# Block 0 of a gated long convolution with a GLU in a new written order: filter basis, condition and loads

## The chip, the cores and the metric

The kernel runs on one core of a Trainium2 chip. The metric is the device time of one execution in microseconds (us); lower is better. A core has TensorE (matrix products; in the profile PE, and PEld for its weight loads), VectorE (DVE), ScalarE (ACT), GpSimd (POOL) and SyncE (SP), which here only issues DMAs.

## The reference, cut to what matters

All data is bf16, with 2048 rows (S), a width D of 576 and a hidden width F of 4608.

```python
mod = silu(c) @ w_mod                        # (1, 6 * 576): sa, ca, ga, sb, cb, gb
h   = layernorm(q) * (1 + ca) + sa
k_shift[s] = sum over t of k[s - 3 + t] * shift_k[:, 3 - t]      # four taps
kv  = k_shift * v
y   = irfft2(rfft2(kv, zero-padded to 4096) * rfft2(ssm_k, padded))[:2048]   # causal long convolution
y   = y + kv * ssm_D
x   = q + ga * (h * y)
h2  = layernorm(x) * (1 + cb) + sb
out = x + gb * ((silu(h2 @ w1) * (h2 @ w3)) @ w2)
```

The condition `c` is one row of 576. Its six products with `w_mod` are needed once, before any row of the result can be finished.

## The kernel before

**Blocks.** The 2048 rows are cut into 8 blocks of 256. For a block, `x_spectrum` multiplies the shifted and gated rows `kv` by a basis of cosines and sines (`Fb`) on TensorE; `w_spectrum` does the same for a block of the filter (`kT`, with the basis `Fk`), each in groups of products whose result is copied out of PSUM. VectorE multiplies the spectra of the blocks that meet in one output block and adds them (`pair`, tiles p and z), and TensorE turns the sum back (`inverse`). A layernorm, the gate and the residual follow; then h2 is written as rows (`h2row`), transposed to columns (`h2T`; by TensorE for blocks 0 and 1, by a transposing DMA in `turn_all` for the others) and modulated by `cbcol` and `sbcol` (1 + cb and sb as columns; `modulate`).

**The GLU.** Four groups of 512 rows, two blocks each, run through `stream(r)` (products of h2T with w1 and w3, which pass through the buffers `wst`) and `down(r)` (products with w2, whose result VectorE multiplies by `gbrow` into `og` and adds to x). Block 0 alone starts the first stream; block 1 joins it later. The convolution of blocks 2 and 3 belongs to the time of stream and down 0, and so on, so that the stream of a group waits for the h2T of its two blocks: the hand-over.

**Two kinds of order.** Nothing is issued at once: each call is recorded, and line 208 (`_Op.emit`), which therefore stands behind every row of the profile, issues it at the end. `setup`, `early_loads` and `first_block` (all of block 0) are emitted in the order in which they are written, engine by engine. From `rec.fixed = False` in `run` on, a planner decides. `weigh` gives each step a due time, `plan` lays the steps out by a model of their lengths, and `search` repeats that `TRIES` times with other random numbers: noise on the due times (`NOISE`), and one of `HOLDS` for how early a load may be issued ahead of its due time. It keeps the order whose modelled time, a mean over the three `CASES`, is smallest. The model adds `WAKE`, 26 ns, from the end of one step to the start of another that waits for it (`lag`). The streams' products are "lanes", whose order is given; all other TensorE work of the planned part is set between them.

**Block 0, step by step.** `setup` makes angles with iotas and integer arithmetic (`angles`, two sets: 1 for the filter basis, 0 for the others) and takes them modulo 2048 (`whole_turns`); ScalarE turns them into bases by sine (`wave`). `taps_waves` makes `Fk`: its first half by sine, its second half as the first times a column of signs, on GpSimd. `early_loads` issues the loads on SP's queue and on ScalarE's; `load_mod(m)` and `load_mod_tail` fetch w_mod's six parts (in the order ga, ca, sa, cb, sb; `load_gb` fetches gb's later). `first_block` then writes, for TensorE: blank products (`warm`); `shift_taps`, which spreads the four taps over the partitions with products of one row; blank products; the filter's spectrum `w_spectrum(0)` between `shifted_rows` (k times the taps on VectorE, shifted and summed by 16 products with a moved identity); `cond` (the silu of c, a row, as five one-row products of 128 columns, which repeat it over 128 columns of `crep`); 16 products of `x_spectrum(0)`; the modulations `mod_piece(2)`, `(1)` and `(0)` (crep times a part of w_mod, 10 products each) around the 24 products of the inverse; `mod_piece(4)` and `(3)` in `mod_columns`, whose rows become columns by twelve small products with four columns each, in two steps of six; the transposes of h2row; and the filter spectrum of block 1.

The blank products and the order of these steps are all that the change touches by hand. Around it stand, on VectorE: k times the taps (p), `kv`, the sums X and V of the spectra and their products z, hg (normalised and gated rows), the residual and the layernorm statistics (`ln_sum` on ScalarE into a tile called junk, `quick_stats`, `ln_square`, `ln_rest`, `ln_bias`).

Of the kernel before, what the change touches and what calls it, by code (L numbers as in the profile page):

```python
# [10 lines left out]
BF16 = mybir.dt.bfloat16  # L11
# [227 lines left out]
class _Recorder:  # L239
# [12 lines left out]
    DOUBT = 900.0  # L252
    PATIENCE = 900.0
    FETCH = 256
    TRIES = 40
    NOISE = 1500.0
    HOLDS = (25000.0, 35000.0, 45000.0, 60000.0)
# [176 lines left out]
    def lag(self, u, v, exact):  # L434
        if v.engine == "sync" and not u.lane and not u.fixed and not exact:
            return v.end + self.DOUBT

        if u.engine == "tensor" and v.engine == "tensor" and v.swap is not u:
            return v.start
        return v.end + self.WAKE  # L440

    def search(self):
# [7 lines left out]
        for n in range(self.TRIES):  # L450
            dice = random.Random(n)
            hold = dice.choice(self.HOLDS) if n else self.HOLD
            for u in self.units:
                u.latest = u.wish + (dice.gauss(0.0, self.NOISE) if n and not u.lane else 0.0)
            try:
                order = self.plan(hold)[1]
            except AssertionError:
                continue
            took = [self.plan(hold, order, *case)[0] for case in self.CASES]
            mean = sum(took) / len(took)  # L460
            if best is None or mean < best[0]:
                best = mean, order
# [242 lines left out]
class _Kernel:  # L705
# [30 lines left out]
    def setup(self):  # L736
# [38 lines left out]
        self.sign = self.small.tile([P, 1], F32, name="sign", tag="sign", bufs=1)  # L775
# [10 lines left out]
        nc.vector.memset(self.one[:], 1.0)  # L786
        nc.vector.tensor_copy(self.acol[:, 0:4], coli[:, 0:4])
        self.ang = {}
        self.angles(nc.vector, 1)
        self.whole_turns(1)  # L790
        nc.vector.tensor_single_scalar(coli[:, 6:7], coli[:, 6:7], 1, op=ALU.bitwise_and)
        nc.vector.tensor_copy(self.acol[:, 4:7], coli[:, 4:7])
        nc.vector.tensor_scalar(self.sign[:], self.acol[:, 6:7], -2.0, 1.0, op0=ALU.mult, op1=ALU.add)
        self.angles(nc.gpsimd, 0)
        nc.gpsimd.memset(self.moved[:, 0:2], 0.0)
        nc.gpsimd.run(lambda: make_identity(self.tc.nc, self.ident), 900.0, (self.ident,))

    def early_loads(self):
        nc = self.nc
        self.crow = self.hp.tile([1, D], BF16, name="crow", tag="u")  # L800
# [3 lines left out]
        self.k0 = self.ld.tile([P, 2, D], BF16, name="kh", tag="kh")  # L804
        nc.scalar.dma_start(self.k0[:], self.k[0:B, :].rearrange("(p c) d -> p c d", c=2))
        nc.scalar.dma_start(self.drow, self.ssm_D.rearrange("(o n) -> o n", o=1))
        self.load_taps(0)
        nc.sync.dma_start(self.crow[:], self.c)
# [3 lines left out]
        self.load_x(0)  # L812
# [28 lines left out]
    def angles(self, engine, which):  # L841
        n = 3 - which
        ang = self.spec.tile([P, n, 2, P], I32, name="ang", tag="V")
        for x in range(n):
# [4 lines left out]
        self.ang[which] = ang  # L849

    def whole_turns(self, which):
        part = self.ang[which][:]
# [6 lines left out]
    def taps_waves(self):  # L859
        self.wave(self.Fk[:, 0:2], self.ang[1][:], 1)  # L860
        self.nc.gpsimd.tensor_scalar(self.Fk[:, 2:4], self.Fk[:, 0:2], self.sign[:, 0:1], 0.0,
                                     op0=ALU.mult, op1=ALU.add)

    def forward_waves(self):
        self.wave(self.Fb[:, 0:2], self.ang[0][:, 0:2], 1)
        self.wave(self.Fb[:, 2:3], self.ang[0][:, 1:2], -1)
# [5 lines left out]
    def inverse_sums(self):  # L872
        nc = self.nc
        for lo, hi, at in ((0, 1, 0), (3, 5, 1)):
            n = hi - lo
            nc.gpsimd.tensor_add(self.Fi[:, at:at + n, 0], self.Fb[:, lo:hi, 0], self.Fb[:, lo:hi, 1])
            nc.gpsimd.tensor_scalar(self.Fi[:, at:at + n, 1], self.Fb[:, lo:hi, 0], -1.0, 0.0,
                                    op0=ALU.mult, op1=ALU.add)
# [14 lines left out]
    def shift_taps(self):  # L893

        nc = self.nc
        for q, (lo, n) in enumerate(((0, 256), (256, 160), (416, 160))):
# [3 lines left out]
            for h in range(2):  # L900
                nc.tensor.matmul(ps[:, h, 0:2 * n], self.one[at, :],
                                 self.shk_raw[at, first + 2 * n * h:first + 2 * n * (h + 1)], start=True, stop=True)
            src = ps[:, :, 0:2 * n].rearrange("p h (d j) -> p j h d", j=4)
# [6 lines left out]
    def cond_silu(self):  # L910
        self.sc = self.hp.tile([1, D], BF16, name="sc", tag="u")
        self.nc.scalar.activation(self.sc[:], self.crow[:], ACT.Silu)

    def cond(self):

        nc, sc = self.nc, self.sc
        self.crep = self.hp.tile([P, 5, P], BF16, name="crep", tag="u")
        pt = self.ps()
        ptv = pt[:].rearrange("p a b -> p (a b)")
        for ct in range(5):  # L920
            n = min(P, D - ct * P)
            nc.tensor.matmul(ptv[:n, ct * P:(ct + 1) * P], sc[0:1, ct * P:ct * P + n], self.one[0:1, :],
                             start=True, stop=True)
        nc.scalar.copy(self.crep[:, 0:4, :], pt[:, 0, :].rearrange("p (a b) -> p a b", a=4))
        nc.scalar.copy(self.crep[0:64, 4, :], pt[0:64, 1, 0:P])
# [13 lines left out]
    def mod_piece(self, m):  # L939
        nc = self.nc  # L940
        p = self.mod_products(m)
# [14 lines left out]
    def mod_columns(self):  # L956
# [8 lines left out]
        for i in range(2):  # L965
            self.warm(1 + i, self.shk[:, 0, 0:512], ps)
# [6 lines left out]
        self.warm(1, self.shk[:, 0, 0:512], ps)  # L973
# [61 lines left out]
    def forward(self, basis, rhs, dst, more=()):  # L1035

        nc = self.nc
        for e in range(2):
            for cs in range(2):
# [3 lines left out]
                if more and e + cs == 0:  # L1043
                    nc.vector.tensor_copy(out, ps[:, :, 0:H])
                else:
                    nc.scalar.copy(out, ps[:, :, 0:H])
# [320 lines left out]
    def first_block(self):  # L1367
# [4 lines left out]
        self.warm(4, blank)  # L1372
        self.shift_taps()
        self.whole_turns(0)
        self.taps_waves()
        self.forward_waves()
        self.cond_silu()
        self.inverse_waves()
        self.warm(6, blank)
        rows = self.shifted_rows()  # L1380
        next(rows)
        spectrum = self.w_spectrum(0)
        next(spectrum)
        next(rows)
        next(spectrum)
        next(rows)
        self.run_all(rows)
        self.cond()
        self.run_all(spectrum)
        self.load_taps(1)  # L1390
        mean, rstd = self.quick_stats(x1[:, 0, :], "l1")
        nmr = self.small.tile([P, 1], F32, name="l1nm", tag="nmr2")
        nc.gpsimd.tensor_mul(nmr[:], mean, rstd)
        nc.gpsimd.tensor_single_scalar(nmr[:], nmr[:], -1.0, op=ALU.mult)
        self.run_all(self.x_spectrum(0))
        self.inverse_sums()
# [4 lines left out]
        self.load_gb()  # L1401
# [3 lines left out]
        ssum, ssq = [self.small.tile([P, 1], F32, name="l1" + k, tag=t) for k, t in (("s", "ssum"), ("q", "ssq"))]  # L1405
        self.ln_sum(x1, 1, 0, ssum[:])
        self.ln_sum(x1, 1, 1, ssq[:])
        self.mod_piece(2)
        nc.vector.tensor_add(X[:, 0, :], X[:, 1, :], X[:, 2, :])
        nc.vector.tensor_mul(z[:, 0:3, :], X[:, 0:3, :], V[:, 0:3, :])  # L1410
        var = self.ln_square(ssum)
        nc.vector.tensor_add(X[:, 3, :], X[:, 4, :], X[:, 5, :])
        r = self.ln_rest(ssq, var)
        nc.scalar.activation(hg[:, 0, :], x1[:, 0, :], ACT.Identity, bias=nmr[:, 0:1], scale=rstd[:, 0:1])
        nc.vector.tensor_mul(z[:, 3:6, :], X[:, 3:6, :], V[:, 3:6, :])
        b = self.ln_bias(ssum, r)
# [16 lines left out]
        nc.scalar.copy(y[:, 0, :].rearrange("p (h d) -> p h d", h=2), ps[0][:, :, 0:H])  # L1433
        nc.vector.tensor_mul(hg[:, 0, :], hg[:, 0, :], y[:, 0, :])
        nc.vector.tensor_add(x1[:, 0, :], x1[:, 0, :], hg[:, 0, :])
        self.residual_row(0, 1, ps[1])
# [3 lines left out]
        columns = self.mod_columns()  # L1440
# [6 lines left out]
        spectrum = self.w_spectrum(1)  # L1447
# [8 lines left out]
        self.run_all(spectrum)  # L1456
# [87 lines left out]
    def conv_second(self):  # L1544
        self.pair_waves()
# [316 lines left out]
```

## Time and profile before

Times are in us. The profiled execution is one more execution than the three timed ones.

| what | value |
|---|---|
| median of three runs | 495.79 (495.44, 495.79, 496.92) |
| profiled execution | 497.05 |
| its span, first to last instruction | 495.3 |
| mean granted TensorE clock | 0.993 |
| bytes moved by DMA | 105.33 MB, 213 GB/s on the mean |
| products of w1 and w3 (2736 of 4693) | 279.4 busy |
| products of w2 (1152) | 144.0 busy |

How to read it. A row of busy time names the engine, its busy time and share of the span, and its count of instructions. A group of instructions is named by engine, operation and tiles: `ps<-h2T,wst` is a product of the tiles h2T and wst into the PSUM tile ps. `<-DVE h2T` behind a group says what ended the idle time ahead of it. A product that uses only 64 of 128 rows runs beside a partner on the other half, so two of them share the time of one. A table of stages gives, for each stretch of time, the busy time and the number of instructions of PE, PEld, DVE, ACT and POOL, then the granted TensorE clock (1.00 is full), the share of time in which the DMA engines were busy, and GB/s. Busy time of an engine that is not the bottleneck costs nothing by itself.

### The profile page before, as it was taken

How to read it: one execution, taken by the hardware profiler on the slowest of the kernel's cores; microseconds unless marked ns; L12 is line 12 of the kernel's file. 1: busy time of each engine (PE TensorE's matmuls, PEld its weight loads, DVE VectorE, ACT ScalarE, POOL GpSimd, SP SyncE). 2: the span in 40 equal slices, each digit the busy share in tenths (PEclk: the TensorE clock that was granted, in tenths of full speed). 3: DMA queues.
4: the chain of work that ended last, by engine and by line, in shares of the span. 5: the costliest groups of instructions: out<-in, count | busy, mean ns of one | idle time of the engine just before them, and what ended most of it. 6: DMA issues, size and time to landing. Idle time of an engine off the chain costs nothing.

```text
span 495.3 us, 11189 instructions
## 1 busy us (share of the span) xinstructions
PE 482.1 (97%) x4693; PEld 298.7 (60%) x4693; DVE 337.0 (68%) x452; ACT 288.1 (58%) x564; POOL 35.8 (7%) x49
## 2 busy tenths in 40 slices
PE   8999989999999999999998999999999999999997
PEld 3667869665777444444776444444777444444775
DVE  6896978999986765997985799999981311112012
ACT  5788458768355657877453366786656355555000
POOL 5520000004020000002020000000000000000000
PEclk9999989999999999999999899999999999999999
DMA  8998954665579999467999899945557354461562
GB/s 231 325 330 281 283 143 124 186 202 177 144 134 303 303 324 343 134 189 251 338 261 295 285 282 306 353 119 175 171 132 190 108 180 148 136 180 59 143 170 71
DMA packets 115196, 105.33 MB, mean 213 GB/s; under 512 B 22533, under 2 KB 108871, under 8 KB 115146
## 3 DMA queue, kind: packets, MB, share of 16 engines
q1 hardware_dynamic: 115000, 104.33, 70.5%
q8 instruction: 36, 0.59, 0.5%
q10 hardware_dynamic: 146, 0.30, 0.2%
q14 instruction: 14, 0.11, 0.1%
HBM read 89.07 MB, written 9.44 MB: 199 GB/s over the span
## 4 chain that ended last, share of the span: by engine, by line
PE 82%; DVE 9%; DMA 3%; ACT 2%; POOL 2%; issue 1%; SPq 0%; DVEq 0%; ACTq 0%
PE ps L208 82%; DVE z L208 3%; DMA wst<-in_B_w_dram 2%; POOL lnr L208 2%; DVE hg L208 1%; DVE p L208 1%; DVE h L208 1%; DMA p<-in_A_shift_k_dram 1%; DVE og L208 1%; DVE spectra L208 1%; DVE x L208 1%; ACT junk L208 1%; ACT h2row L208 0%; DVE h2T L208 0%; ACT hg L208 0%
## 5 line engine op out<-in xcount | busy, mean ns | idle before, releaser
L208 PE MATMUL ps<-h2T,wst 64*128 64x512 bf16 (+1 forms) x2736 | 279.4, 355 | 2.1 <-DVE h2T L208 2.0
L208 PEld LDWEIGHTS <-wst 64*128 64x128 bf16 x2736 | 135.9, 94 | 125.7 <-DVE h2T L208 2.5
L208 PE MATMUL ps<-wst,h 128*128 128x288 bf16 x1152 | 144.0, 286 | 0.5 <-DMA wst<-in_B_w_dram 0.4
L208 PEld LDWEIGHTS <-h 128*128 128x128 bf16 x1152 | 112.4, 98 | 31.0 <-issue 2.6
L208 ACT ACTIVATE h<-ps 128x512 bf16<-128x512 f32 x144 | 86.4, 600 | 53.7 <-PE ps L208 53.3
L208 ACT CAST u<-ps 128x512 bf16<-128x512 f32 x146 | 84.7, 581 | 54.8 <-PE ps L208 54.5
L208 DVE TENSOR_TENSOR h<-h,u 128x1024 bf16<-128x1024 bf16 x72 | 49.6, 689 | 78.3 <-ACT u L208 41.3
L208 DVE TENSOR_TENSOR p<-spectra 128x3456 bf16<-128x3456 bf16 x28 | 54.7, 1953 | 5.0 <-DMA spectra<-Vd 4.8
L208 DVE TENSOR_TENSOR z<-z,p 128x3456 bf16<-128x3456 bf16 x28 | 54.7, 1953 | 0.2
L208 ACT ACTIVATE junk<-x 128x576 bf16<-128x576 bf16 x56 | 38.4, 686 | 24.0 <-DVE x L208 23.4
L208 POOL TENSOR_TENSOR lnr<-lnv,neghalf 128x2 f32<-128x2 f32 x13 | 19.3, 1488 | 305.4 <-DVE lnv L208 304.8
L208 DVE TENSOR_TENSOR og<-ps,gbrow 128x576 bf16<-128x576 f32 (+1 forms) x18 | 12.4, 690 | 37.1 <-PE ps L208 36.5
L208 DVE TENSOR_TENSOR spectra<-spectra 128x1152 bf16<-128x1152 bf16 (+1 forms) x35 | 25.8, 737 | 2.1 <-ACT spectra L208 1.6
L208 ACT CAST spectra<-ps 128x576 bf16<-128x576 f32 x33 | 21.0, 650 | 2.9 <-PE ps L208 2.9
L208 PEld LDWEIGHTS <-Fb 64*128 64x128 bf16 (+1 forms) x236 | 14.9, 95 | 11.5 <-DVE z L208 3.3
L208 ACT ACTIVATE h2row<-x,lnn,lnr 128x576 bf16<-128x576 bf16 (+1 forms) x24 | 14.5, 644 | 12.5 <-DMA h2T<-h2row 7.5
L208 PE MATMUL ps<-h2T,spectra 64*128 64x256 bf16 x288 | 19.3, 282 | 0.4 <-DVE h2T L208 0.4
L208 PE MATMUL ps<-kT,Fk 64*128 64x288 bf16 (+1 forms) x124 | 19.2, 294 | 0.5 <-ACT h2T L208 0.5
L208 DVE TENSOR_TENSOR z<-z 128x1152 bf16<-128x1152 bf16 x26 | 19.3, 750 | 0.1
L208 PE MATMUL ps<-kv,Fb 64*128 64x288 bf16 (+1 forms) x136 | 18.5, 284 | 0.1
L208 DVE TENSOR_TENSOR p<-kh,shk 128x3456 bf16<-128x3456 bf16 (+1 forms) x8 | 15.0, 1876 | 2.9 <-DMA kh<-in_A_k_dram 2.9
L208 PEld LDWEIGHTS <-spectra 64*128 64x128 bf16 x288 | 15.5, 98 | 2.3 <-DVE h2T L208 0.6
(106 smaller groups left out, 278.6 us busy)
## 6 DMA issues: line engine op xcount, KB each, us to landing
wst<-in_B_w_dram SPq DMA_DIRECT2D x72, 512.0 KB, 4.8
wst<-in_B_w_dram SPq DMA_DIRECT2D x72, 288.0 KB, 3.4
kh<-in_A_k_dram SPq DMA_DIRECT2D x7, 720.0 KB, 6.7
wst<-in_B_w_dram SPq DMA_DIRECT2D x72, 64.0 KB, 3.8
spectra<-Xd SPq DMA_DIRECT2D x5, 864.0 KB, 6.3
spectra<-Vd SPq DMA_DIRECT2D x5, 864.0 KB, 6.7
Xd<-spectra SPq DMA_DIRECT2D x4, 864.0 KB, 5.6
Vd<-spectra SPq DMA_DIRECT2D x4, 864.0 KB, 4.9
```

What stands on the lines that cost most here:

```text
L208: getattr(getattr(nc, self.engine), self.method)(*[_real(a) for a in self.args], **{k: _real(v) for k, v in self.kw.items()})
```

## The change

It has two parts: block 0 is written in another order with some of its steps made in another way, and the planner's search gets other numbers.

In block 0:

- **Bases.** The second half of `Fk` is made by ScalarE, as a second sine of the same angles with a scale and a bias that are columns (`sgn`, two columns of plus or minus pi/1024 and pi). The angles of set 0 are made by GpSimd (four of six) and VectorE (two of six), inside `setup`, where `whole_turns` now stands in two pieces; the sines of `Fb` come apart (`forward_waves(0)`, `(1)`).
- **Loads.** c goes first on ScalarE's queue, ahead of k and ssm_D, instead of SP's. On SP's queue x comes ahead of v, where it stood behind v, the ga part of w_mod and a tail.
- **Condition.** c lies in partition 64 of a wider tile with a zero tail. Five one-row products of four columns, in the PSUM tile of the last taps, make it a column per 128; ScalarE takes the silu of these 128 x 5 values; GpSimd multiplies them, repeated, with ones into `crep` (128 x 640). Before, ScalarE took the silu of the row of 576, five products of 128 columns spread it and two ScalarE copies of PSUM followed.
- **TensorE's order.** Seven blank products in front for four, two behind the taps for six. All groups of `w_spectrum(0)` in one run ahead of all the shifting products; their copies all by ScalarE. `mod_products(2)` ahead of `x_spectrum(0)`. In `mod_columns` one blank product for four; the first group of `w_spectrum(1)` stands ahead of its two steps as before, the second now between them; the other two groups move behind the end of block 0, into `conv_second`, as do the loads of gb.
- **Small steps.** The layernorm sums of x's second half stand earlier; the shifted mean `nmr` is one VectorE instruction for two of GpSimd; `inverse_sums` comes in two pieces; both halves of the inverse are copied by ScalarE (`residual_row` did the second on VectorE from PSUM).

In the planner: 60 tries for 40, other `HOLDS`, no noise on SP's steps, and a constant `CARE` for `WAKE` where a planned TensorE step waits; both are 26 ns.

```diff
-    TRIES = 40
+    TRIES = 60
-    HOLDS = (25000.0, 35000.0, 45000.0, 60000.0)
+    HOLDS = (45000.0, 60000.0, 80000.0)
...
+        if u.engine == "tensor" and not u.lane and not u.fixed and not exact:
+            return v.end + self.CARE
         return v.end + self.WAKE
...
-                u.latest = u.wish + (dice.gauss(0.0, self.NOISE) if n and not u.lane else 0.0)
+                u.latest = u.wish + (dice.gauss(0.0, self.NOISE) if n and not u.lane and u.engine != "sync" else 0.0)
...
+        nc.vector.memset(self.crow[64:65, D:5 * P], 0.0)
-        self.angles(nc.vector, 1)
-        self.whole_turns(1)
+        self.angles(nc.vector, 1, range(2))
+        self.whole_turns(1, 0, 2)
-        nc.vector.tensor_scalar(self.sign[:], self.acol[:, 6:7], -2.0, 1.0, op0=ALU.mult, op1=ALU.add)
-        self.angles(nc.gpsimd, 0)
+        for i, x in enumerate((math.pi / 1024, -math.pi)):
+            nc.vector.tensor_scalar(self.sgn[:, i:i + 1], self.acol[:, 6:7], -2.0 * x, x, op0=ALU.mult, op1=ALU.add)
+        self.angles(nc.gpsimd, 0, range(2))
+        self.angles(nc.vector, 0, range(2, 3))
...
+        self.whole_turns(0, 0, 2)
+        self.whole_turns(0, 2, 3)
     def early_loads(self):
...
+        nc.scalar.dma_start(self.crow[64:65, 0:D], self.c)
         nc.scalar.dma_start(self.k0[:], self.k[0:B, :].rearrange("(p c) d -> p c d", c=2))
         nc.scalar.dma_start(self.drow, self.ssm_D.rearrange("(o n) -> o n", o=1))
         self.load_taps(0)
-        nc.sync.dma_start(self.crow[:], self.c)
+        self.load_x(0)
         self.load_v(0)
         self.load_mod(2)
         self.load_mod_tail(0, 3)
-        self.load_x(0)
...
     def taps_waves(self):
         self.wave(self.Fk[:, 0:2], self.ang[1][:], 1)
-        self.nc.gpsimd.tensor_scalar(self.Fk[:, 2:4], self.Fk[:, 0:2], self.sign[:, 0:1], 0.0,
-                                     op0=ALU.mult, op1=ALU.add)
+        self.nc.scalar.activation(self.Fk[:, 2:4], self.ang[1][:], ACT.Sin, bias=self.sgn[:, 1:2],
+                                  scale=self.sgn[:, 0:1])
...
+            if q == 2:
+                self.cond(ps[:, 0, 384:404])
...
-        self.sc = self.hp.tile([1, D], BF16, name="sc", tag="u")
-        self.nc.scalar.activation(self.sc[:], self.crow[:], ACT.Silu)
...
+        for ct in range(5):
+            nc.tensor.matmul(ps[:, 4 * ct:4 * ct + 4], self.crow[64:65, ct * P:(ct + 1) * P], self.one[64:65, 0:4],
+                             start=True, stop=True)
+        scol = self.small.tile([P, 5], BF16, name="scol", tag="scol", bufs=1)
+        nc.scalar.activation(scol[:], ps[:, 0:20:4], ACT.Silu)
         self.crep = self.hp.tile([P, 5, P], BF16, name="crep", tag="u")
-        pt = self.ps()
-        ptv = pt[:].rearrange("p a b -> p (a b)")
-        for ct in range(5):
-            n = min(P, D - ct * P)
-            nc.tensor.matmul(ptv[:n, ct * P:(ct + 1) * P], sc[0:1, ct * P:ct * P + n], self.one[0:1, :],
-                             start=True, stop=True)
-        nc.scalar.copy(self.crep[:, 0:4, :], pt[:, 0, :].rearrange("p (a b) -> p a b", a=4))
-        nc.scalar.copy(self.crep[0:64, 4, :], pt[0:64, 1, 0:P])
+        nc.gpsimd.tensor_tensor(self.crep[:], _ap(self.one, 0, [[0, 5], [1, P]]), _ap(scol, 0, [[1, 5], [0, P]]),
+                                op=ALU.mult)
...
-    def mod_columns(self):
+    def mod_columns(self, more):
...
-            self.warm(1 + i, self.shk[:, 0, 0:512], ps)
+            if i == 0:
+                self.warm(1, self.shk[:, 0, 0:512], ps)
+            else:
+                next(more)
...
-        self.warm(1, self.shk[:, 0, 0:512], ps)
...
-                if more and e + cs == 0:
-                    nc.vector.tensor_copy(out, ps[:, :, 0:H])
-                else:
-                    nc.scalar.copy(out, ps[:, :, 0:H])
+                nc.scalar.copy(out, ps[:, :, 0:H])
...
     def first_block(self):
-        self.warm(4, blank)
+        self.taps_waves()
+        self.forward_waves(0)
+        self.warm(7, blank)
         self.shift_taps()
-        self.whole_turns(0)
-        self.taps_waves()
-        self.forward_waves()
-        self.cond_silu()
-        self.inverse_waves()
-        self.warm(6, blank)
+        self.forward_waves(1)
+        self.warm(2, blank)
         rows = self.shifted_rows()
         next(rows)
-        spectrum = self.w_spectrum(0)
-        next(spectrum)
-        next(rows)
-        next(spectrum)
-        next(rows)
-        self.run_all(rows)
-        self.cond()
-        self.run_all(spectrum)
+        self.run_all(self.w_spectrum(0))
+        ssum, ssq = [self.small.tile([P, 1], F32, name="l1" + k, tag=t) for k, t in (("s", "ssum"), ("q", "ssq"))]
+        self.ln_sum(x1, 1, 0, ssum[:])
+        self.ln_sum(x1, 1, 1, ssq[:])
+        self.inverse_waves()
+        mean, rstd = self.quick_stats(x1[:, 0, :], "l1")
+        next(rows)
+        next(rows)
+        self.run_all(rows)
         self.load_taps(1)
+        self.inverse_sums(0)
...
-        nc.gpsimd.tensor_mul(nmr[:], mean, rstd)
-        nc.gpsimd.tensor_single_scalar(nmr[:], nmr[:], -1.0, op=ALU.mult)
+        nc.vector.scalar_tensor_tensor(nmr[:], mean, -1.0, rstd, op0=ALU.mult, op1=ALU.mult)
...
+        ga = self.mod_products(2)
         self.run_all(self.x_spectrum(0))
-        self.inverse_sums()
...
-        self.load_gb()
...
-        self.residual_row(0, 1, ps[1])
+        for cc in range(2):
+            nc.scalar.copy(y[:, cc, :].rearrange("p (h d) -> p h d", h=2), ps[cc][:, :, 0:H])
+            nc.vector.tensor_mul(hg[:, cc, :], hg[:, cc, :], y[:, cc, :])
+            nc.vector.tensor_add(x1[:, cc, :], x1[:, cc, :], hg[:, cc, :])
...
-        columns = self.mod_columns()
+        self.spectrum = spectrum = self.w_spectrum(1)
+        columns = self.mod_columns(spectrum)
...
-        spectrum = self.w_spectrum(1)
         next(spectrum)
...
-        self.run_all(spectrum)
...
     def conv_second(self):
+        yield from self.spectrum
+        self.load_gb()
         self.pair_waves()
```

## The prediction, made before the result was known

> **What bounds the kernel now.** I read the share of busy time first, then what TensorE waits for, then the busy time by stages, then the order of time at the places found.
>
> The page's first part and TensorE's waits (engine, tile, releaser: us in total, times, longest):
>
> ```profile
> PE 482.1 (97%) x4693; PEld 298.7 (60%) x4693; DVE 337.0 (68%) x452; ACT 288.1 (58%) x564; POOL 35.8 (7%) x49
> ...
> PE ps L208 <- DVE h2T L208: 3.6, 3, 2.0
> PE ps L208 <- DVE z L208: 2.0, 2, 1.1
> PE ps L208 <- DVE h2row L208: 1.0, 1, 1.0
> PE ps L208 <- DVE bnmv L208: 0.9, 1, 0.9
> ...
> PE ps L208 <- DMA wst<-in_B_w_dram: 0.4, 2, 0.3
> ```
>
> TensorE is the bound, and its idle time is under ten us, nearly all of it a wait for VectorE at a hand-over from one pair of blocks to the next. So the change can pay in three ways: fewer products, less idle time, less time at half clock. The stages (TensorE, weight loads, VectorE, ScalarE, GpSimd busy us; granted clock; DMA share; GB/s) show the last:
>
> ```profile
> 3.90:7.40 3.50, 3.49 (x13) 1.02 (x13) 2.45 (x3) 2.41 (x4) 0.92 (x5) 1.00 0.98 220
> 7.40:10.83 3.43, 3.43 (x15) 1.67 (x14) 2.53 (x3) 1.87 (x5) 2.26 (x1) 1.00 1.05 325
> ...
> 61.70:65.30 3.60, 1.28 (x14) 0.67 (x12) 2.90 (x11) 2.26 (x6) 0.93 (x2) 1.00 0.69 153
> 65.30:68.90 3.60, 3.58 (x34) 2.74 (x36) 3.57 (x5) 0.44 (x2) 0.00 (x0) 0.53 0.05 15
> ...
> 270.70:272.80 2.10, 0.10 (x3) 0.03 (x2) 2.00 (x6) 0.00 (x0) 0.00 (x0) 1.00 0.91 358
> 272.80:277.10 4.30, 4.30 (x25) 1.63 (x26) 4.25 (x5) 0.15 (x1) 0.00 (x0) 0.60 0.90 302
> ```
>
> Behind each of the two long holes (61.7 to 65.3, 270.7 to 272.8) TensorE runs some 3.4 us at half clock: 1.7 us lost beside the hole. The first two rows print no grant (1.00 is a blank there); the spacing of products tells it: 240 ns for 288 columns until 10.8 us, 122.5 ns after.
>
> In block 0 the chain of waits is TensorE alone from 3.91 to 29.4 us. Its order of time (start, us, what):
>
> ```profile
> 1.17 1.89 PE L208 MATMUL ps<-h2T 128*128 128x512 bf16 x4 [1.17 <-DVE h2T L208]
> 3.91 1.01 PE L208 MATMUL ps<-p,one 1*128 1x512 bf16 x6 [0.84 <-DMA p<-in_A_shift_k_dram]
> 4.85 2.74 PE L208 MATMUL ps<-h2T 128*128 128x512 bf16 x6
> 7.38 1.16 PE L208 MATMUL ps<-kT,Fk 128*128 128x288 bf16 x4
> 8.48 0.65 PE L208 MATMUL ps<-knat,Fk 1*128 1x288 bf16 x2
> ```
>
> **The change, part by part.** First block 0, walked along TensorE with these spacings.
>
> Warm-up. Seven blank products in front instead of four: 1.17 + 7 x 0.427 = 4.16, so the taps start 0.25 us after their data (3.91); they take 0.94: 5.10. The condition's five products have four columns instead of 128: as the six of the columns step (0.30 in place of 0.50). Two blank products instead of six: 0.85: 6.25. Then the filter groups in one run. One half is four products 1.10, two one-row products 0.59, four products 0.96, so 2.65; two halves at half clock end at 11.55, or 11.2 with the clock up at 10.83 as now. Their factors are ready: the first basis takes ScalarE 0.735 and now comes before the copies of the taps (angles ready at 3.0, so about 3.8), the second, with a pointer for scale too, 0.74 to 0.9 (two-pointer rows: 0.855 against 0.727 for hg and junk), about 4.7. That replaces 2.66 us of GpSimd. Behind these ScalarE still has Fb 0.72, the taps' copies 0.69 twice and the condition 0.2, so VectorE's first product p starts near 6.7 instead of 6.56; it ends by 9.4 with z, and the shifting products want them at 11.2.
>
> From there at full clock: 16 shifting products 1.96 (13.2), the gate's modulation 1.43 (14.6), 16 of the x spectrum 1.96 (16.55), two modulations 2.86 (19.4), 24 inverse products 2.95 (22.35; now 23.60), two modulations 2.86 (25.2), four filter products 0.5, one blank 0.39, six 0.30, four filter products in place of two blanks 0.5, six 0.30: 27.2 (now 28.7). What must be in time for that: v, behind x in the queue by 288 KB, lands near 8.2 instead of 7.36 and is wanted at 12.5; the first modulation's weights near 10.2 and 11.4 instead of 9.30 and 10.46, wanted at 13.2; k, behind c on ScalarE's queue, 0.4 later, at 3.9, wanted at 6.7. The shifted mean on VectorE is 0.15 us for GpSimd's 0.70 and 0.61. All covered; uncovered, each costs its own lateness.
>
> The tail: the last copy of a filter product ends near 27.7, columns 28.0, ScalarE's four h2T 1.5 us: 29.5 (now 30.99). Eight filter products instead of twelve then stand before the stream, which starts at 29.8 instead of 31.90: **-2.1 us**. VectorE leaves block 0 only 1.4 us earlier (29.7 for 31.08).
>
> The condition by GpSimd is weighed against a rule. The row: two-input Wo took 0.602 for 128 columns and 0.927 for 256, so 640 make 1.9 us. The Trainium skill (GPSIMD Engine Reference, 1. Specifications) says GpSimd shares its SBUF interfaces with VectorE and contends with two-input instructions there, and p and z run just then. The trace knows such a case: a 128x2 power took 4.89 us at 113.4 beside products, else 0.56. Held until z ends (9.4), it would be done by 11.4, wanted at 13.2: nothing on the path by either.
>
> The clock is the second. The Trainium skill (TensorE: Matmul & The Clock Gate, Part 1) lets one busy window of 3.4 us lift the half clock. With TensorE busy from 1.17 on, that is at most 8.0 instead of 10.83, worth another 1.4 us. The row speaks against it: 3.49 of 3.50 us busy, and half clock still in the next 3.43. If one-row products don't count, the new run has 1.17 us of them where the old had 0.59, and the lift may come a window later, 14.2: 1.7 us lost. I take 10.83 and keep -1.4 and +1.7.
>
> Block 1. VectorE's row of work from 31 to 65.8 sets its h2T; nothing is added to it, so it ends with VectorE's 1.4 us. The gate weights' loads (650 KB) go behind, so the stream's weights come no later. TensorE had the gbrow modulation (1.43) in mid-stream and the next pair's filter products (1.0) after the hole; both now stand in the hole. So after block 1 TensorE is **2.3 us** ahead (1.4 and about 0.9). I leave the half clock behind the hole as it is, with 1.7 us to win.
>
> Blocks 2 and 3 (118 to 135). From block 1's h2T on, VectorE's rows up to the second inverse add up to 64.6 us for TensorE's 62.5; before 64.2 for 64.0, or 67.1 for 65.5 at its second half. TensorE arrives ahead and waits: **+0.7**.
>
> The hand-over at 272:
>
> ```profile
> 269.83 0.76 DVE L208 TENSOR_TENSOR og<-ps,gbrow 128x576 bf16<-128x576 f32 x1 [0.54 <-PE ps L208]
> 270.63 0.46 DVE L208 TENSOR_TENSOR x<-x,og 128x576 bf16<-128x576 bf16 x1
> 271.19 0.76 DVE L208 TENSOR_TENSOR og<-ps,gbrow 128x576 bf16<-128x576 f32 x1
> 271.86 1.36 DVE L208 TENSOR_SCALAR h2T<-h2T,cbcol,sbcol 128x256 bf16<-128x256 bf16 x5
> ```
>
> All five modulations of h2T stand behind two output products that wait for TensorE's own last product, so the hole of 2.0 us is made by the order. In the new order four of the five, those of the columns that the stream takes first among them, stand ahead of both, and the fifth behind one: 0.76 + 0.3 less the 0.43 that the first products last, a hole of 0.6, too short for the clock (0.93 and 1.11 at 119 and 134 did not drop it). 1.4 + 1.7, rounded down: **-3.0**. It holds if h2T's two transposing loads have landed; they are issued 16 to 32 products further ahead of the end than before. The rest (149 to 238 and 277 to 492) is full.
>
> Sum: -2.3 + 0.7 - 3.0 = -4.6. The profiled execution took 497.05 with a span of 495.3 (1.75 around it) and lies 1.26 above the median; on its own time 492.5, on the median of 495.79 **491.2 us**.
>
> **Rivals.** 0.3% is 1.5 us, about what a measurement of this kernel can tell from no change: 494.3 to 497.3 is "same".
>
> *The hand-over does not close*, because the loads land late or a pair's product ahead of the modulations waits for a spectrum, as p did for 4.8 us at 265. Then 495.79 - 2.3 + 0.7 = 494.2; with the late clock 495.9, no change. For it: that wait. Against: the spectrum is issued 46 products earlier.
>
> *The clock alone*: early 489.8, late 492.9; with the hole in block 1 kept warm 489.5.
>
> *Slower*: TensorE takes the next pair's filter products ahead of block 1's transposes, and those behind it wait in line. Their kT comes by a transposing load and four copies, issued at 48.1 and 54.4 to 56.8 now; landing near 59 even so. The transposes are due near 60.7, and every us that kT is late there moves VectorE and TensorE alike. From landings after 66.5 on it eats the 5.8 us that lie between the forecast and 497.3; at 68, 498.7. Against: those loads wait for room that a stream two us earlier gives back earlier.
>
> **How the numbers follow.** As forecast, either clock: 0.62 (488.8 to 493.2). Hand-over open: 0.26, of which 0.14 in "same". Slower order: 0.12. Faster 0.74, same 0.14, slower 0.12. The range leaves 0.1 below and 0.1 above: 488.7 (early clock and a warm hole) to 497.4.
>
> **What would show it.** Stream start at 29.8; full clock at 10.8; filter groups without a pause; one blank product ahead of the first columns step, four filter products between the two; at the end of the second down pass a hole under 1 us and no half clock behind it. The forecast is wrong if the hole at 272 stays, if a new wait of over 2 us stands on TensorE before 150 us, or if half clock lasts to 14 us.

## The result

The changed kernel takes 492.38 us (median of 15 runs, 489.41 to 495.74), the kernel before 495.79 (15 runs, 494.05 to 496.95). The ratio is 0.9928 with a 95% interval of 0.9906 to 0.9950: 3.6 us faster, give or take 1.1. The forecast was 491.2 with a range of 488.7 to 497.4. The profiled execution took 492.71, with a span of 490.9 (before: 497.05 and 495.3).

The page's first part and TensorE's waits after the change (engine, tile, releaser: us in total, times, longest):

```profile
PE 477.5 (97%) x4681; PEld 297.3 (61%) x4681; DVE 336.6 (69%) x457; ACT 289.4 (59%) x565; POOL 25.7 (5%) x45
...
PE ps L208 <- DMA wst<-in_B_w_dram: 2.7, 5, 0.8
PE ps L208 <- DVE h2T L208: 1.9, 2, 1.2
PE ps L208 <- DVE z L208: 1.8, 3, 0.8
PE ps L208 <- DMA kT<-in_A_ssm_k_dram: 0.9, 2, 0.6
PE ps L208 <- ACT h2T L208: 0.8, 2, 0.4
PE ps L208 <- DMA kT<-knat: 0.4, 1, 0.4
```

The wait for VectorE's h2T has halved (3.6 before). What has grown is the wait for weights of the down passes, from 0.4 to 2.7 us: now the largest.

Block 0 in order of time (start, us, what), TensorE, then one row each of ScalarE and GpSimd:

```profile
1.17 3.17 PE L208 MATMUL ps<-h2T 128*128 128x512 bf16 x7 [1.17 <-DVE h2T L208]
4.27 0.60 PE L208 MATMUL ps<-p,one 1*128 1x512 bf16 x6
...
5.71 0.65 PE L208 MATMUL ps<-kT,Fk 128*128 128x288 bf16 x4 [0.30 <-DMA kT<-in_A_ssm_k_dram]
...
8.82 1.14 PE L208 MATMUL ps<-p,moved 128*128 128x288 bf16 x8
...
23.72 0.66 PE L208 MATMUL ps<-kT,Fk 128*128 128x288 bf16 x4 [0.62 <-DMA kT<-in_A_ssm_k_dram]
...
28.44 3.78 PE L208 MATMUL ps<-h2T,wst 64*128 64x256 bf16 x66
```

```profile
4.03 0.81 ACT L208 ACTIVATE Fk<-spectra,sgn 128x512 bf16<-128x512 int32 x1
```

```profile
6.21 1.25 POOL L208 TENSOR_TENSOR u<-one,scol 128x640 bf16<-128x640 bf16 x1 [2.13 <-ACT scol L208]
```

The stream starts at 28.44 instead of 31.90:

```profile
31.90 0.28 PE L208 MATMUL ps<-h2T,wst 64*128 64x256 bf16 x2
```

The record of the granted clock says full from 4.22 us on (10.83 before), and the six tap products show it.

The hand-over of groups 1 and 2, TensorE first, before and after:

```profile
272.77 12.05 PE L208 MATMUL ps<-h2T,wst 64*128 64x512 bf16 x94 [2.00 <-DVE h2T L208]
284.65 0.29 PE L208 MATMUL ps<-kT,Fk 64*128 64x288 bf16 x2
```

```profile
246.68 13.88 PE L208 MATMUL ps<-wst,h 128*128 128x288 bf16 x112 [0.74 <-DMA wst<-in_B_w_dram]
261.34 8.00 PE L208 MATMUL ps<-wst,h 128*128 128x288 bf16 x64 [0.79 <-DMA wst<-in_B_w_dram]
269.28 6.00 PE L208 MATMUL ps<-h2T,wst 64*128 64x512 bf16 x54
```

Then VectorE after the change:

```profile
265.24 1.12 DVE L208 TENSOR_SCALAR h2T<-h2T,cbcol,sbcol 128x256 bf16<-128x256 bf16 x4 [0.72 <-DMA h2T<-h2row]
268.40 0.76 DVE L208 TENSOR_TENSOR og<-ps,gbrow 128x576 bf16<-128x576 f32 x1 [2.04 <-PE ps L208]
269.08 0.34 DVE L208 TENSOR_SCALAR h2T<-h2T,cbcol,sbcol 128x256 bf16<-128x256 bf16 x1
269.88 0.76 DVE L208 TENSOR_TENSOR og<-ps,gbrow 128x576 bf16<-128x576 f32 x1
```

Four modulations stand ahead of the output products, the fifth behind one, and the stream (269.28) starts without a hole. Ahead of it stand two new holes, for w2.

**Where the time went.** For a lead I count the TensorE work that is still to come (columns of its products at the spacing of full clock) and compare the times at which two traces have the same amount left. Against the kernel before, in us, at seven such places, named by the time in the trace of before (nothing changes after the last):

| profiled execution of | 32 | 72 | 136 | 231 | 267 | 281 | 391 |
|---|---|---|---|---|---|---|---|
| the change | -3.5 | -3.9 | -4.5 | -3.1 | -1.4 | -5.2 | -4.7 |
| e3: old kernel, hand-over turned | +0.4 | +0.3 | +0.3 | -0.2 | +0.7 | -3.1 | +1.2 |
| e5: the same, kT loads too | -1.5 | -0.6 | -0.6 | -0.8 | -0.2 | -4.0 | -4.0 |
| e6: new block 0, old order | -2.5 | -2.8 | -2.8 | -2.6 | -0.9 | -2.6 | -1.7 |
| e7: e6 and e5's two edits | -0.5 | -0.6 | -0.6 | +0.2 | +0.5 | -3.3 | -3.2 |
| e12: the change, one-row blanks in front | -1.8 | -3.7 | -4.3 | -2.6 | -1.8 | -5.6 | -5.1 |

The profiled execution of before lies 1.26 us above its median, so the -4.7 in the last column stands for some -3.4 against that median.

### The profile page after: what moved, and what is told of

Read it like the earlier page. It is cut to its first block, busy times and chain, and to the rows that moved or that the text cites. A ratio compares the mean times of both kernels' runs of the same rounds, so it can differ in the third digit from the quotient of the medians.

```text
span 490.9 us, 11182 instructions
## 1 busy us (share of the span) xinstructions
PE 477.5 (97%) x4681; PEld 297.3 (61%) x4681; DVE 336.6 (69%) x457; ACT 289.4 (59%) x565; POOL 25.7 (5%) x45
## 4 chain that ended last, share of the span: by engine, by line
PE 67%; DVE 15%; ACT 7%; DMA 6%; issue 2%; SPq 1%; POOL 1%; POOLq 0%; DVEq 0%; ACTq 0%
PE ps L208 67%; DVE z L208 5%; DMA wst<-in_B_w_dram 3%; DVE p L208 2%; ACT h2row L208 2%; DVE spectra L208 1%; DMA kT<-in_A_ssm_k_dram 1%; SPq L208 1%; DVE h L208 1%; DVE hg L208 1%; DVE kv L208 1%; DVE x L208 1%; DMA kT<-knat 1%; POOL lnr L208 1%; ACT u L208 1%
## 5 line engine op out<-in xcount | busy, mean ns | idle before, releaser
L208 POOL TENSOR_TENSOR lnr<-lnv,neghalf 128x2 f32<-128x2 f32 x13 | 13.9, 1073 | 308.5 <-DVE lnv L208 308.5
L208 PE MATMUL ps<-kT,Fk 64*128 64x288 bf16 (+1 forms) x116 | 17.4, 285 | 2.4 <-DMA kT<-in_A_ssm_k_dram 0.9
L208 DVE TENSOR_TENSOR z<-spectra 128x3456 bf16<-128x3456 bf16 (+1 forms) x9 | 15.8, 1763 | 2.0 <-DMA spectra<-Vd 1.9
```

The source lines that it names most:

```text
L208: getattr(getattr(nc, self.engine), self.method)(*[_real(a) for a in self.args], **{k: _real(v) for k, v in self.kw.items()})
```

## The experiments

All were timed beside the kernel before on the same chip. Where a run "holds the order", the planner's result (order and PSUM places) was written into the kernel as a list in place of the search.

**e1 and e2: the two halves apart.** The new block 0 with the old planner numbers, and the old block 0 with the new ones.

```diff
 # e1, on the changed kernel; e2 is the reverse, on the kernel before
-    TRIES = 60
-    HOLDS = (45000.0, 60000.0, 80000.0)
+    TRIES = 40
+    HOLDS = (25000.0, 35000.0, 45000.0, 60000.0)
...
-                u.latest = u.wish + (dice.gauss(0.0, self.NOISE) if n and not u.lane and u.engine != "sync" else 0.0)
+                u.latest = u.wish + (dice.gauss(0.0, self.NOISE) if n and not u.lane else 0.0)
```

> The changed kernel with the planner's old numbers (40 tries, the old four holds, noise on SP's steps too): block 0 as changed, everything behind it drawn anew. Both parts pay (my account): stream start at 28.4 us, since block 0 is untouched; this draw has all five modulations of h2T ahead of both output products at the hand-over of groups 1 and 2 too, so no hole there, and about 492 us. Only the planner's numbers pay, and block 0's lead is lost to VectorE on the way: about 495.8. Only block 0 pays: 492, but then the old block 0 with the new numbers must stay at 495.8.

Measured: 494.63 us, ratio 0.9956 (0.9932 to 0.9980). That is none of the times expected. There is no hole at 272, but one of 2.40 us at 156, for a w2 weight, and 3.4 us at half clock behind it. TensorE's waits for these weights:

```profile
PE ps L208 <- DMA wst<-in_B_w_dram: 4.4, 4, 2.4
```

> The kernel before with the planner's new numbers (60 tries, holds of 45, 60 and 80 us, no noise on SP's steps): block 0 as before. Both parts pay: stream start at 31.9 us as before, no hole at the hand-over of groups 1 and 2 (five modulations ahead of both output products in this draw): 495.8 less 3.0 to 3.7, so 492.1 to 492.8. The hand-over is worth nothing at the end, since TensorE only arrives earlier at its next wait: 495 to 496.

Measured: 497.04 us, ratio 1.0017 (0.9989 to 1.0045). No hole at 272 here either, since both orders have the modulations ahead of the output products; yet e2 gains nothing. A w2 weight holds TensorE up for 2.77 us at 261, and the clock is at half from 260.56 to 263.97:

```profile
261.15 11.32 PE L208 MATMUL ps<-wst,h 128*128 128x288 bf16 x80 [2.77 <-DMA wst<-in_B_w_dram]
```

So another draw of the planner brings holes of its own. e1 lies 1.4 us above the change by the two ratios (0.9956 and 0.9928), though their intervals overlap, and a difference between two draws can't be put down to the edit that led to them. From here on the order was held.

**e3 and e5: the hand-over alone**, in the kernel before.

```diff
 # VectorE's order at the hand-over of groups 1 and 2 (e3, e5)
+h2T<-h2T,cbcol,sbcol  x5
 og<-ps,gbrow
 x<-x,og
 og<-ps,gbrow
-h2T<-h2T,cbcol,sbcol  x5
 x<-x,og
 # SP's order there (e5 alone)
 spectra<-Xd
+kT<-knat  x4
 wst<-in_B_w3  wst<-in_B_w1  x2
 spectra<-Xd
-kT<-knat
 spectra<-Xd
-kT<-knat  x2
 wst<-in_B_w3  wst<-in_B_w1
-kT<-knat
```

> The kernel before, every order held, except that at the hand-over of groups 1 and 2 VectorE's five modulations of h2T stand ahead of both output products instead of behind them. The step of the forecast: the hole of 2.0 us and the half clock behind it (1.7 us) go, the 1.36 us of modulations delay the two output products, which no product of TensorE wants at once: 492.1 to 492.8 us, span 491.5 to 492.3. The rival: TensorE then runs 3.7 us ahead into waits for VectorE's next pair or for weights, and the time is 494.5 or more.

Measured: 497.28 us, ratio 1.0013 (0.9990 to 1.0035): nothing. The hole at 272 is gone, and 10 us later a longer one begins:

```profile
271.44 10.32 PE L208 MATMUL ps<-h2T,wst 64*128 64x512 bf16 x94
284.23 0.42 PE L208 MATMUL ps<-kT,Fk 64*128 64x288 bf16 x2 [2.47 <-DMA kT<-knat]
```

TensorE came to the next block's filter products sooner, and their loads stand in SP's queue behind loads that wait for buffers (the last of the four is issued at 278.26). The hole dropped the clock there instead (284.03 to 287.45).

> The kernel before, every order held, with the five modulations ahead of both output products (as in the run with that alone) and with the four small loads of the next filter block (kT from knat) moved from behind the stream's weights and two spectra to ahead of them, where SP stands idle at 267.7. If the hand-over's gain was taken back only by those loads (the wait of 2.47 us at 284 and the half clock behind it): no wait there, 492.1 to 492.8 us. If TensorE meets another late load instead, the memory traffic being full: 494.5 or more.

Measured: 492.79 us, ratio 0.9943 (0.9925 to 0.9961), 2.8 us faster than before.

```profile
270.51 10.32 PE L208 MATMUL ps<-h2T,wst 64*128 64x512 bf16 x94
280.66 0.29 PE L208 MATMUL ps<-kT,Fk 64*128 64x288 bf16 x2
```

No wait is left at the filter products. So the closed hand-over is worth 2.8 us, if what TensorE meets next has landed.

**e8: the hand-over in the changed kernel**, turned back.

```diff
 # VectorE's order at the hand-over, the rest held
-h2T<-h2T,cbcol,sbcol  x4
 og<-ps,gbrow
-h2T<-h2T,cbcol,sbcol  x1
 x<-x,og
 og<-ps,gbrow
+h2T<-h2T,cbcol,sbcol  x5
 p<-spectra
```

> The changed kernel, every order held, except that at the hand-over of groups 1 and 2 the five modulations of h2T go back behind both output products, as in the kernel before. If the closed hand-over is worth what the forecast said, here where the next filter products find their loads landed: a hole of 2 us near 269 and half clock behind it, 495.5 to 496.1 at the end. If TensorE's next wait takes it up: 492.4 to 493.5.

Measured: 494.88 us, ratio 0.9980 (0.9961 to 0.9999), 2.6 us above the change by the two ratios.

```profile
271.15 4.06 PE L208 MATMUL ps<-h2T,wst 64*128 64x512 bf16 x36 [2.25 <-DVE h2T L208]
```

The hole is back, and in this execution the clock stayed up behind it, so that less than the 3.7 us expected was lost. The clock changes only at the edges of a grid of 3.41 us (last section). Most of this hole fell into one window, 267.45 to 270.86, with TensorE busy for 1.45 us of it; in the kernel before, the window from 270.24 to 273.65 had 1.41 us, and there the clock fell. Where the limit lies these two can't show.

**e6 and e7: block 0 alone, and with the hand-over.** The changed kernel's block 0 with the planned order of the kernel before behind it. The steps that the change moves out of block 0 stand first there: two filter groups and the gb loads.

```diff
 # e6, on the changed kernel: the planned order of the kernel before
+wst<-in_B_w_mod  x3
+ps<-kT,Fk (a group)  W<-ps  ps<-kT,Fk (a group)  W<-ps
 # then as planned before; e7 has e5's two edits besides
```

> Block 0 as changed, with the planned order of the kernel before held behind it (its two filter groups and the gb loads, which the change moves out of block 0, stand first). Block 0 alone: the stream starts at 28.4 to 29.1 us (31.9 before), the holes at 62 to 65 and at 272 stay as before, and the lead of 2.5 to 3.5 us lasts: 492.3 to 493.3. If VectorE or the loads set the pace behind block 1, the lead is gone by 150 us: 495 to 496.

Measured: 495.42 us, ratio 0.9991 (0.9974 to 1.0007): no difference that could be told from none.

```profile
247.99 21.87 PE L208 MATMUL ps<-wst,h 128*128 128x288 bf16 x176 [1.09 <-DMA wst<-in_B_w_dram]
271.85 10.36 PE L208 MATMUL ps<-h2T,wst 64*128 64x512 bf16 x94 [1.99 <-DVE h2T L208]
282.91 0.29 PE L208 MATMUL ps<-kT,Fk 64*128 64x288 bf16 x2 [0.70 <-DMA kT<-knat]
```

The lead of 2.5 us stands until 231, then loads take 1.5 us of it (0.42 at 242 and 1.09 at 248 for 0.15 before), and the filter loads another 0.70: they land when SP's queue comes to them, not when TensorE is ready. That the table shows a lead of 2.6 us again between the two is the clock: this execution's hole at 272 lay across an edge of the grid (270.50), and no half clock followed.

> Block 0 as changed, the planned order of the kernel before behind it, and at 272 us both edits of the run with the modulations and the four loads moved. If the two gains add: 488.6 to 489.8. If one of them is taken back by late loads: 492 to 493.

Measured: 491.99 us, ratio 0.9924 (0.9905 to 0.9944). Against e5 the new block 0 adds 0.2%, with intervals that overlap: not clear of noise. The gain is about that of the change itself, with none of its planned order. The profiled execution had no lead from block 0 at all, because its clock came up late:

```profile
4.27 1.03 PE L208 MATMUL ps<-p,one 1*128 1x512 bf16 x6
...
7.16 0.66 PE L208 MATMUL ps<-knat,Fk 1*128 1x288 bf16 x2
...
11.30 2.13 PE L208 MATMUL ps<-p,moved 128*128 128x288 bf16 x8
```

The shifting products start at 11.30 for the change's 8.82, and the full clock is granted only at 13.65.

**e4 and e12: what lifts the clock.**

```diff
 # e4, the changed kernel, order held
-        self.warm(7, blank)
+        self.warm(4, blank)
...
-        self.warm(2, blank)
+        self.warm(5, blank)
 # e12, the changed kernel, order held: one row in place of 128
-        self.warm(7, blank)
+        self.warm(7, self.h2T[0][0:1, 0, :])
```

> The changed kernel, the order behind block 0 held, with four blank products in front (as before) and five behind the taps (seven and two in the change). If TensorE's clock came up at 4.2 us because the seven kept it busy for 3 us without a pause: now a pause of some 0.8 us ahead of the taps, full clock only at about 7.6 or 11, stream start 29.8 instead of 28.4, and 0.5 to 1.4 us more at the end (what VectorE's hand-over at block 1 passes on). If the clock comes up by something else: still full by 4.3 us, stream start 28.5 to 29.0 (three more products behind the taps, at 0.21 us).

Measured: 493.29 us, ratio 0.9928 (0.9902 to 0.9953), as the change. The taps had landed early in this execution, so there was no pause ahead of them; full clock came at 7.17, and the stream started at 28.39. The expected loss of 0.5 to 1.4 us at the end is not there, but without the pause this execution is no test of it.

> The changed kernel, its order held, with the seven blank products in front made of one row each (same 512 columns, same time, a sum over one partition instead of 128). If the clock comes up behind a stretch of 3.41 us that is more than three quarters filled with products of all rows, and one-row products don't count (as the runs so far read): TensorE is as busy as before, but full clock comes at 8.4 us or later, never at 4 to 5 (four of the eight runs with seven full-row blanks had it at 4.2 to 4.6), and the stream starts at 29 or later; at the end up to 1 us more than the changed kernel on the mean. If any busy TensorE counts: full clock between 3.8 and 7.3 us.

Measured: 492.40 us (six runs, 492.19 to 492.57), ratio 0.9927 (0.9903 to 0.9952). Busy time in the three windows ahead of the full clock (from:to, us; PE, PEld, DVE, ACT, POOL busy with counts; clock, where 1.00 is a blank here too; DMA share; GB/s):

```profile
1.20:4.60 3.40, 3.40 (x18) 1.43 (x18) 3.09 (x18) 2.06 (x3) 2.53 (x10) 1.00 0.59 145
4.63:8.05 3.42, 3.42 (x12) 1.14 (x11) 2.82 (x4) 2.80 (x7) 1.25 (x1) 1.00 0.98 274
8.05:11.46 3.41, 3.41 (x16) 1.65 (x14) 2.99 (x6) 1.64 (x4) 0.27 (x1) 1.00 1.08 290
```

TensorE was wholly busy from 1.2 us on, and the clock stayed at half until 11.46: products of one row don't lift it. The stream started at 30.06, 1.6 us later than in the change. Block 1's first products were as late (64.25 for 62.64), but in the change's execution 3.4 us at half clock followed (62.25 to 65.66), and here none; the ends are equal.

**e9, e10 and e11: loads moved in SP's queue.** e9 and e10 start from e1, e11 from the change.

```diff
 # e9: SP's order in the first down pass of e1
+wst<-in_B_w2 (the last)
 kh<-in_A_k
-wst<-in_B_w2 (the last)
 Xd<-spectra
 # e10 besides, in the second
+wst<-in_B_w2
 h2T<-h2row
-wst<-in_B_w2
+wst<-in_B_w2
 spectra<-Vd
-wst<-in_B_w2
 # e11: the change, at 140 to 148 (two w2 loads and four kT loads ahead of transposing loads)
+wst<-in_B_w2
 h2T<-h2row
-wst<-in_B_w2
-h2T<-h2row
 wst<-in_B_w2
 kT<-knat  x2
 wst<-in_B_w2
 kT<-knat  x2
+h2T<-h2row
 # and at 242 and 253
-Xd<-spectra
 wst<-in_B_w2  x2
+Xd<-spectra
...
-spectra<-Vd
 wst<-in_B_w2
+spectra<-Vd
```

> The first run (changed block 0, old planner numbers), its order held, with one load moved: the last w2 load of the first down pass goes ahead of the load of k and the store of a spectrum, behind which it stood (as it does in the changed kernel's own order). If block 0's lead was lost there to a weight that came late behind 1.6 MB of other data: the hole of 2.4 us at 156 and the half clock behind it (1.7 us) go, and 494.6 becomes 490.5 to 491.5. If the memory is simply full there: the hole moves to the next load, and the time stays within 1 us of 494.6.

Measured: 493.06 us, ratio 0.9923 (0.9894 to 0.9952), for e1's 0.9956. The hole of 2.4 us at 156 and the half clock behind it are gone; a shorter wait stands ahead of it:

```profile
152.79 0.65 PE L208 MATMUL ps<-kT,Fk 128*128 128x288 bf16 x4 [1.35 <-DMA kT<-knat]
```

About 1.6 us of the 4.1 came through by the two ratios, with intervals that overlap. (The load had stood behind the load of k alone, issued at 147.29 and 147.92; the store of the spectrum followed it, at 148.37.)

> The same with two more w2 loads moved, in the second down pass: one ahead of a transposing load that waits for its rows, one ahead of a spectrum of 864 KB. The holes of 0.78 and 0.95 us at 250 and 253 go: 1.0 to 1.7 us less than with the first load alone, 489 to 490.5. If the spectrum that now lands later holds VectorE up at the hand-over of groups 1 and 2, the gain is given back there.

Measured: 492.52 us, ratio 0.9933 (0.9905 to 0.9961): nothing beyond e9. The two holes became three, of 0.39, 0.38 and 0.66 us.

> The changed kernel, its order held, with the same kind of edit: w2 loads ahead of the transposing loads that wait for rows at 140 to 144, the four small kT loads earlier, a stored spectrum behind two w2 loads at 242, a loaded one behind a w2 load at 253. Its waits for w2 and kT (0.45, 0.40 and 0.43 us at 146 to 152, 0.74 at 247, 0.79 at 261) shrink to under 1 us in sum: 490 to 491 instead of 492.4. If they only move: 492 to 493.

Measured: 494.71 us, ratio 0.9958 (0.9934 to 0.9982), by the ratios 1.5 us worse than the change, with intervals that overlap. The w2 waits at 146 to 149 are gone, and TensorE and ScalarE show what came in their place:

```profile
154.18 1.17 PE L208 MATMUL ps<-kT,Fk 128*128 128x288 bf16 x4 [2.19 <-ACT W L208]
```

```profile
151.04 2.56 ACT L208 ACTIVATE h2T<-h2T,sbcol,cbcol 128x256 bf16<-128x256 bf16 x5 [9.78 <-DMA h2T<-h2row]
153.51 0.61 ACT L208 CAST W<-ps 128x576 bf16<-128x576 f32 x1
```

The second transposing load, now behind the kT loads, landed at 151.02. ScalarE waited for it at the head of its queue (147.15 in the change), with the copies of the filter products behind, and TensorE waited for those copies: a hole of 2.19 us and half clock again. None of these versions is clearly faster than the change.

## Why the prediction was right, and where it was not

- **The sum** (-4.6, so 491.2) came out as -3.4 at the median. Its largest term held. Two others did not, with opposite signs: that the sum is only 1.2 us off is in part luck, and the range was so wide that it held "no change" too.
- **Block 0, -2.1** (stream at 29.8 instead of 31.90). Right at equal clock: with full clock from 9.19 (e1) the stream starts at 29.10; the old block, by its four traces (7.75 and 7.97 give 30.45 and 30.52; 10.83 and 10.97 give 31.90 and 32.28), would start near 31.1 then. The second basis took 0.81 (forecast 0.74 to 0.9), GpSimd's 640 columns 1.25 (forecast 1.9; done at 7.46, not at 11.4 as if held until z ends). But the forecast weighed only a GpSimd that is held. It was VectorE's p, begun 0.53 later, that took longer:

```profile
6.74 1.94 DVE L208 TENSOR_TENSOR p<-kh,shk 128x2304 bf16<-128x2304 bf16 x1 [0.61 <-PE ps L208]
8.60 1.35 DVE L208 TENSOR_TENSOR z<-kh,shk 128x2304 bf16<-128x2304 bf16 x1
```

The second product, of the same size, took 1.35, and so did p in all four traces of the old block (1.93 to 1.94 in all ten of the new). No run isolates it. With the early clock the first products with p and with z came 0.25 and 0.20 us later than the spacing, which the forecast had put at nothing.

- **The clock, taken at 10.83, -1.4 or +1.7.** Both ends occurred: 4.22 in the change's profiled execution (28.44, 1.4 us earlier than forecast), 13.41 and 13.65 in e9 and e7 (31.07 and 31.40). The rule weighed there, by which one busy window lifts the clock at 8.0 or sooner, fails in e1, e7, e9 and e12 (9.19 to 13.65); that one-row products don't count, the reason given against it, is shown by e12. What the forecast missed is that the time differs from execution to execution; the page weighed there (the Trainium skill, TensorE: Matmul & The Clock Gate, Part 1) says that the window runs free of the kernel's start, and the traces agree (last section). At the end the clock's lift left no trace that could be told: e12, without the rows that lift it early, has the change's ratio (0.9927 and 0.9928).
- **After block 1, -2.3.** The profiled execution had 2.7 at block 1's first products, here before and after:

```profile
65.32 2.39 PE L208 MATMUL ps<-h2T,spectra 64*128 64x256 bf16 x20 [0.43 <-DVE h2T L208]
62.64 6.11 PE L208 MATMUL ps<-h2T,spectra 64*128 64x256 bf16 x82 [0.70 <-DVE h2T L208]
```

But the step that failed is the one behind it: "The rest (149 to 238 and 277 to 492) is full", with -2.3 carried to the end. e6 shows block 0's lead alone come to 0.1%: loads with a place in SP's queue took much of it back in the down passes (-2.6 to -0.9), and where the clock came up late there was little to begin with (e7: -0.5). Such waits were not in the sum at all. In the change itself e8 shows how little is left: with the hand-over turned back it is 1.0 us faster than the kernel before (0.9961 to 0.9999), and that is block 0 and all other planned order together. A w2 load is issued when its buffer comes free and has the 16 products of each of three other buffers before its own turn: 3 x 1.96, 5.9 us. Issued at 254.71 beside 864 KB of a spectrum it took 6.59, and TensorE waited 0.79. Before, the same kind of load cost 0.15 and 0.27.
- **Blocks 2 and 3, +0.7.** It did not come: the waits for z there are 1.8 us in sum (three), for 2.0 before (two). In its place, 1.3 us of waits for w2 and kT at 146 to 152.
- **The hand-over at 272, -3.0.** Right, by 2.6 (e8) to 2.8 us (e5), and for the stated reason as far as the hole goes (none was left, 0.6 was forecast). The 1.7 us of half clock in the sum are not paid by every execution: e8's profiled one had the hole at full clock, and the mean clock of the 23 executions of the kernel before beside e5 goes from 0.990 to 0.999, where one window at half makes 0.0035. The forecast gave it one condition, that h2T's loads have landed. e3 shows the one that was missing: what TensorE meets next, the filter products of the next block, must have its loads as well. In the change these stand behind the first 154 products of the stream (94 before) and found theirs landed; in the old order they gave everything back.
- **The rivals.** "Slower", by the filter products ahead of block 1's transposes, happened in small: TensorE waited 0.37 there, for ScalarE's copies of the first transposes. "The clock alone" named times from 489.5 to 492.9; the 15 runs spread over 489.4 to 495.7, 6.3 us for 2.9 before the change. Two figures of "slower" are off by a little: from 491.2 to 497.3 it is 6.1 us, not 5.8, and a landing at 68 makes 498.5, not 498.7.

## What to carry to other kernels

When a hole at a hand-over is closed, go on along the bound engine's order to the next product that waits for a load, and ask whether that load can come earlier; if its place in the queue is fixed, the hole only moves. A lead won early is kept only as far as the first load whose time is set by buffers and queue order rather than by the engine that leads. And where a planner with random tries orders the rest, hold its order to measure an edit, since another draw alone can move the time by as much.

## What the runs showed of the hardware

The granted clock changes only at the edges of a grid of 3.413 us, which lies differently against the start in every execution. In the trace of before the times 10.83, 65.44, 68.85, 273.65 and 277.07 lie 16, 1, 60 and 1 such windows apart. For every window ahead of the full clock I worked out from the order of time what share lies under products of all 128 rows, each counted until the next product starts (the last one or two windows before the lift; earlier ones are emptier or have at most 0.72):

| trace | window without a lift: share (busy in all) | window that lifted: its end, share |
|---|---|---|
| before | 4.00 to 7.41: 0.75 (1.00) | 10.83, 0.83 |
| the change | none | 4.22, 0.89 |
| e1 | 2.37 to 5.78: 0.72 (1.00) | 9.19, 0.83 |
| e2 | 1.14 to 4.56: 0.55 (0.80) | 7.97, 0.97 |
| e3 | 4.14 to 7.55: 0.62 (0.90) | 10.97, 0.83 |
| e4 | 0.35 to 3.76: 0.53 (0.76) | 7.17, 0.94 |
| e5 | 0.92 to 4.34: 0.55 (0.70) | 7.75, 0.87 |
| e6, e8, e11 | none | 4.26, 4.62 and 4.51, 0.90 to 0.91 |
| e7 | 6.82 to 10.24: 0.69 (1.00) | 13.65, 0.96 |
| e9 | 6.58 to 9.99: 0.76 (1.00) | 13.41, 0.89 |
| e10 | none | 5.01, 0.78 |
| e12 | 1.22 to 4.63: 0.00 (1.00), 4.63 to 8.05: 0.69 (1.00) | 11.46, 0.83 |

In these 14 traces a window of 0.78 and more lifted the clock, and one of 0.76 and less did not, however busy TensorE was. The limit itself is no sharper than the count: with each product taken to its modelled end, e9's window that did not lift and e10's that did are both at 0.80. That rows count at all is shown: e12 took them away and nothing else, and its window from 1.22 to 4.63, wholly busy, did not lift, where e8's from 1.21 to 4.62 did. The seven blank products of the change fill a window only if an edge falls well, and its one-row products spoil the next one or two if not: a lift anywhere from 4.2 to 13.7 us, where the old block had 7.8 to 11.0.

That the wider spread of the change's runs comes from this is argued, not shown: the runs without a profile don't record the lift. Their mean clock counts only the half clock behind it, and that is not the source alone: the six runs at 1.00 lie between 489.41 and 493.77. For the lift as the source speaks that e12's six runs lie within 0.38 us of each other; against it, that their median is the change's.
